# Windowed attention with a cosine feed-forward on one core: a pair's load one slot sooner, the scale of v one and two slots later

## The chip, the cores and the metric

The kernel runs on one core of a Trainium2 chip. The metric is the device time of one execution in microseconds (us). The engines of the core are PE (TensorE, matmuls; PEld is its weight load), DVE (VectorE), ACT (ScalarE), POOL (GpSimd) and SP (SyncE, which issues the DMAs here).

## The reference

Attention of 8 batches, 8 heads, 512 local and 32 global tokens of 64 dimensions; local queries see the global keys and a window of 32 to each side, global queries see all. Its output, 4608 tokens by 512, goes through a feed-forward layer whose activation is h cos(h):

```python
s_g = scale * np.matmul(q_g, k_all.transpose(0, 1, 3, 2))
out_g = np.matmul(sm(s_g), v_all)
s_ll = np.where(np.abs(pos[:, None] - pos[None, :]) <= 32, scale * q_l @ k_l^T, -1e9)
s_lg = scale * np.matmul(q_l, k_g.transpose(0, 1, 3, 2))
out_l = np.matmul(sm(np.concatenate([s_lg, s_ll], axis=-1)), np.concatenate([v_g, v_l], axis=2))
...
x = concatenate([out_g, out_l]) as (4608, 512)
h = x @ w_in            # 512 x 2048
out = (h * np.cos(h)) @ w_out   # 2048 x 512
```

## The kernel before, in words

Every fp32 operand of a product is scaled by a power of two and split into a high and a low fp16 part, and a product is three matmuls (high by high, high by low, low by high). Heads go in pairs: a batch has 4 pairs, 0 to 3. The feed-forward layer takes chunks of 256 tokens, two to a batch, and a chunk takes 8 steps (two 128-wide pieces of the 2048 each). A step is a *slot*, so a batch has 16 slots.

What belongs to a pair, by names and lines. `load_qk` (L457) fetches queries and keys, 608 KB, into `qkr`, of which there is one buffer. `qk_a` takes their largest magnitude, `qm` (L497, DVE). `qk_b` spreads it over the partitions through PE (`d_qk` L473 on DVE, `pm_qk` L479 on PE) and `qk_c` makes the scale `qs` of it. `qk_d` splits: `qa` (L537, ACT) and then `kl` (L538, DVE), the last reader of `qkr`. `qk_e` rearranges the parts by DMA (`kh<-qa`, L547 and L548; `qa<-kl`, L550; `kl<-kl`, L552). The scores `ps` are matmuls (L606, L607) in four windows, DVE masks them into `t` (L623, two halves to a window, with a maximum `mn`), ACT takes exponentials (L446), ACT and DVE write them out as `planes` (L702, L705), four DMA transposes a pair turn these into `pt` (L717), and PE multiplies them with v into `acc` (L750), which is split into `xh` (L775, ACT) and `xl` (L776, DVE). The global queries have their own scores (`gps`, `gt` L815), transposes (`ptg` L843) and product `gacc`.

What belongs to a batch's v: `load_v` (L464) fetches it, 1280 KB, into `vr` (one buffer). `v_a` takes the maximum `vm` (L566, DVE) and makes `d_v` (L473); `v_b` spreads it through PE (`pm_v`, L479); `v_c` takes the scale `vs` (L576 and three small instructions that follow it, DVE); `v_d` splits v of one pair, `vh` (L596, ACT) and `vl` (L597, DVE).

A step j of a chunk c: 24 matmuls `ph` (L919), `u` on ACT (L941) and DVE (L942), the sine `w` (ACT, L446), its square (POOL, L954), `gf` = (w - 0.5) ph (DVE, L956, the last reader of `ph`, which has 3 buffers), `gh` (ACT, L960), `gl` (POOL, L961), and matmuls `po` (L975 to L977). After a chunk, `o` (L983 on DVE, L985 on ACT) is written out. Exponential and sine need different tables on ACT, so an ACT_TABLE_LOAD stands between groups of them. The pieces of `w_out` are split in the same way in the first 250 us (L231, L268, L281).

What sets the order. The program is written as `at(slot, phase, function, arguments)`. Slot and phase give each call a priority; a list scheduler then places the instructions of each engine by priority and by its own estimate of when their operands are ready. Each engine, and SP with its DMAs, works through its own list in order. Names such as PF, PG, PA or PJ are phases inside a slot, from PA0, the first, to PJ, the last. For batch b from 2 on, t = 16 (b - 1) + T0 with T0 = 3, and pair p is placed around t + 4p: the load at `s_load`, the maximum at `s_qa` = -12, the splitting at `s_qd` = -10, the scores at -7 to -4, the transposes at -1, the product with v at 0, the splitting of v at -8. `s_v` = -12 places the load of v. Only pair 0 of batch 2 has a load of its own, at t - 11. In names with numbers, `qkr_4_0` is pair 0 of batch 4, `u_5_3` is step 3 of chunk 5, `t_3_3_2` is window 2 of pair 3 of batch 3; the last number only counts tiles.

Of the kernel before, what the change touches and what calls it, by code (L numbers as in the profile page):

```python
# [77 lines left out]
LVK = -1  # L78
LQK = -1
QMA = 2  # L80
s_load = -13
s_qa = -12
s_qd = -10
s_qe0 = -9
# [16 lines left out]
s_v = -12  # L101
# [36 lines left out]
def body(tc, qk, v, wi, wo, mask, out):  # L138
# [5 lines left out]
    with ExitStack() as ctx:  # L144
# [15 lines left out]
        for i in range(4):  # L160
            t = cp.tile([P, 2, 2, 256], F16, name=f"planes{i}")
# [844 lines left out]
        def at(slot, phase, f, *a, pr=None):  # L1006
            e = (phase, len(ev[slot]), f, a)
            ev[slot].append(e)
            pr = (slot, phase) if pr is None else pr if isinstance(pr, tuple) else (pr, phase)
            rank[slot, e[1]] = pr + (slot, e[1])  # L1010
# [3 lines left out]
        def attn_pair(b, p, o):  # L1014
            at(o["load"], PJ, load_qk, b, p)
            at(o["qa"], PF, qk_a, b, p)
            if o["tight"] or QB == 0:
                at(o["qa"], PG, qk_b, b, p)
                at(o["qa"], PG2, qk_c, b, p)
            else:  # L1020
                at(o["qa"] + 1, PA, qk_b, b, p)
                at(o["qa"] + 1, PB, qk_c, b, p)
            at(o["qd"], PF2, qk_d, b, p)
            for k in range(3):
                at(o["qe"][k], PA0 if k == 0 or o["tight"] else PJ, qk_e, b, p, k)
            for i in range(4):
                at(o["sc"][i], PA, sc_a, b, p, i)
                at(o["sc"][i], PA if o["tight"] else PC, sc_b, b, p, i)
                at(o["ex"], PI, sc_c, b, p, i)
                at(o["sd"], PF, sc_d, b, p, i)  # L1030
                at(o["tr"][i], PA2, sc_e, b, p, i)
            at(o["vd"], PF2, v_d, b, p)
            at(o["av"], PA, av_a, b, p)
            at(o["av"] if b else -6, PF, av_b, b, p)
            if p % 2:
                g = p // 2
                for k in range(2):
                    at(o["gs"][k], PA, g_a, b, g, k)
                    at(o["gs"][k], PA if o["tight"] else PC, g_b, b, g, k)
                at(o["ex"], PI, g_c, b, g)  # L1040
                at(o["gd"], PF2, g_d, b, g)
                at(o["ge"], PA2, g_e, b, g)
                at(o["gf"] if b else GF0, PG, g_f, b, g)
                at(o["gf"] if b else GF0, PH2, g_g, b, g)

        def steady(t, late=False):
            o = dict(
                load=t + s_load, qa=t + s_qa, qd=t + s_qd, qe=(t + s_qe0, t + s_qe1, t + s_qe2),
                sc=[t + s_sc0, t + s_sc1, t + s_sc2, t + s_sc3], ex=t + s_ex, sd=t + s_sd,
                tr=(t + s_tr,) * 4, vd=t + s_vd, av=t + s_av, gs=(t + s_gs0, t + s_gs1),  # L1050
                gd=t + s_gd, ge=t + s_ge, gf=t + s_gf, tight=False,
            )
            if late:
                o |= dict(load=t - 11, qa=t - 10, qd=t - 9, qe=(t - 8,) * 3)
            return o
# [45 lines left out]
        for b in range(2, B):  # L1101
            t = 16 * (b - 1) + T0
            at(t + s_v, PA0, load_v, b)
            at(t + s_v + 1, PF, v_a, b)
            at(t + s_v + 1, PG, v_b, b)
            at(t + s_v + 1, PG2, v_c, b)
            for p in range(NPAIR):
                attn_pair(b, p, steady(t + 4 * p, b == 2 and p == 0))
        ma, mb, mc, md, m2, ob, oc = (
# [99 lines left out]
```

## Time and profile before

| | before |
|---|---|
| median of 3 runs (lowest, highest) | 1033.6 us (1032.02, 1034.86) |
| the profiled execution | 1034.44 us, span 1032.6 us, mean granted clock 0.954 |
| busy: PE, PEld, DVE, ACT, POOL | 893.3, 609.2, 710.7, 717.9, 461.8 us |
| share of the chain that ended last | PE 33%, DVE 28%, ACT 15%, DMA 11%, POOL 5%, issue 5% |
| in that chain: DMA `qkr<-qk`, DVE `qm` | 7%, 2% |
| DMA | 120.19 MB, mean 116 GB/s |
| a `qkr` load | 608.0 KB, median 4.8 us from issue to landing |

Up to about 300 us the first two batches and the weights are prepared; up to about 814 us attention of batches 3 to 7 runs beside the feed-forward layer, at some 107 us a batch; behind that only the feed-forward layer is left. "Idle before" an instruction is time in which its engine stood still, and the name behind the arrow is what it waited for.

### The profile page before, as it was taken

The page shows a single profiled execution, that of the slowest core. Times are in us where ns is not written, and L with a number is a line of the kernel's source. Part 1 is how long each engine was busy: PE and PEld are TensorE (multiplying, and loading weights), DVE is VectorE, ACT ScalarE, POOL GpSimd, SP SyncE. Part 2 cuts the span into 40 slices and gives each one's busy share as a digit, 9 for nine tenths or more (in the row PEclk, how much of TensorE's full clock was granted, in tenths as well). Part 3 has the DMA queues.
Part 4 walks back from the last instruction along what each step waited for, and adds up shares of the span by engine and source line. Part 5 has one row for each costly group of instructions (what it writes and reads, how often), then busy time and mean ns, then how long its engine had stood idle before and what let it go on. Part 6 is the DMA issues. An engine that isn't in the chain of part 4 may idle for free.

```text
span 1032.6 us, 21117 instructions
## 1 busy us (share of the span) xinstructions
PE 893.3 (87%) x7947; PEld 609.2 (59%) x7947; DVE 710.7 (69%) x1811; ACT 717.9 (70%) x1468; POOL 461.8 (45%) x494
## 2 busy tenths in 40 slices
PE   1245878769999999899899999999989999999996
PEld 0134645444666766666666666666666667766663
DVE  4999786897477777867777777868777766433231
ACT  5788798785577776877687768777777876544342
POOL 3696477984233333333334324343333343534442
PEclk9996979788999999999999999999989999999998
DMA  9796145775254464454645354545536452100000
GB/s 361 269 303 246 15 142 142 181 164 139 70 103 111 103 157 108 99 115 97 147 93 119 91 145 93 122 91 153 111 81 109 107 88 61 34 21 22 1 21 21
DMA packets 165822, 120.19 MB, mean 116 GB/s; under 512 B 143064, under 2 KB 143064, under 8 KB 163672
## 3 DMA queue, kind: packets, MB, share of 16 engines
q1 hardware_dynamic: 165720, 118.85, 46.3%
q8 instruction: 62, 1.02, 0.4%
q14 instruction: 40, 0.33, 0.1%
HBM read 56.00 MB, written 8.91 MB: 63 GB/s over the span
## 4 chain that ended last, share of the span: by engine, by line
PE 33%; DVE 28%; ACT 15%; DMA 11%; POOL 5%; issue 5%; SPq 1%; ACTq 0%; DVEq 0%; POOLq 0%
PE ph L919 13%; DMA qkr<-qk 7%; PE po L975 5%; PE po L976 5%; PE po L977 5%; DVE planes L705 4%; DVE t L623 4%; DVE u L942 3%; ACT L446 3%; ACT planes L702 3%; ACT t L446 3%; DMA vr<-v 2%; DVE kl L538 2%; POOL w L954 2%; DVE qm L497 2%
## 5 line engine op out<-in xcount | busy, mean ns | idle before, releaser
L919 PE MATMUL ph<-xh,wi_h 128*128 128x256 f16 x1024 | 281.9, 276 | 10.0 <-DVE gf L956 9.8
L919 PE MATMUL ph<-xl,wi_h 128*128 128x256 f16 x1024 | 282.1, 275 | 0.0
L919 PE MATMUL ph<-xh,wi_l 128*128 128x256 f16 x1024 | 282.0, 275 | 0.0
L961 POOL TENSOR_TENSOR gl<-gf,gh 128x512 f16<-128x512 f32 x136 | 167.2, 1233 | 236.5 <-ACT gh L960 236.5
L954 POOL TENSOR_TENSOR w<-w 128x512 f32<-128x512 f32 x136 | 141.5, 1044 | 266.0 <-ACT w L446 266.0
L919 PEld LDWEIGHTS <-wi_h 128*128 128x128 f16 x2176 | 211.8, 99 | 52.3 <-issue 12.4
L975 PE MATMUL po<-wo_h,gh 128*128 128x512 f16 x544 | 206.5, 384 | 28.2 <-DVE o L983 17.1
L976 PE MATMUL po<-wo_l,gh 128*128 128x512 f16 x544 | 209.6, 385 | 10.6 <-POOL wo_l L231 10.6
L977 PE MATMUL po<-wo_h,gl 128*128 128x512 f16 x544 | 209.5, 386 | 0.0
L446 ACT ACTIVATE w<-u,ca 128x512 f32<-128x512 f32 x136 | 97.8, 721 | 109.9 <-DVE u L942 109.3
L942 DVE SCALAR_TENSOR_TENSOR u<-u,cm,ph 128x512 f32<-128x512 f32 x136 | 100.9, 742 | 97.3 <-ACT u L941 97.3
L446 ACT ACTIVATE t<-t,mn 128x192 f32<-128x192 f32 (+1 forms) x256 | 116.9, 458 | 49.3 <-DVE mn L623 48.9
L956 DVE SCALAR_TENSOR_TENSOR gf<-w,ph 128x512 f32<-128x512 f32 x136 | 92.6, 682 | 58.3 <-POOL w L954 58.1
L960 ACT CAST gh<-gf 128x512 f16<-128x512 f32 x136 | 83.1, 611 | 69.8 <-DVE gf L956 59.2
L919 PEld LDWEIGHTS <-wi_l 128*128 128x128 f16 x1088 | 107.5, 99 | 15.1 <-issue 1.4
L623 DVE CUSTOM_DVE_ANT_0 t<-ps,msk,al 128x192 f32<-128x192 f32 (+1 forms) x256 | 99.5, 426 | 11.7 <-PE ps L607 11.2
L941 ACT ACTIVATE u<-ph,cm 128x512 f32<-128x512 f32 x136 | 92.1, 678 | 21.4 <-PE ph L919 19.5
L977 PEld LDWEIGHTS <-gl 128*128 128x128 f16 x544 | 53.8, 99 | 75.5 <-issue 13.9
L705 DVE SCALAR_TENSOR_TENSOR planes<-t,sm,planes 128x224 f16<-128x224 f32 (+1 forms) x198 | 88.6, 496 | 10.7 <-ACT planes L702 10.7
L976 PEld LDWEIGHTS <-gh 128*128 128x128 f16 x544 | 53.7, 99 | 70.7 <-issue 22.7
L975 PEld LDWEIGHTS <-gh 128*128 128x128 f16 x544 | 53.1, 98 | 62.8 <-issue 14.5
L702 ACT ACTIVATE planes<-t,sm 128x192 f16<-128x192 f32 (+1 forms) x196 | 74.3, 453 | 0.0
(185 smaller groups left out, 1427.7 us busy)
## 6 DMA issues: line engine op xcount, KB each, us to landing
qkr<-qk SPq DMA_DIRECT2D x29, 608.0 KB, 4.8
vr<-v SPq DMA_DIRECT2D x8, 1280.0 KB, 7.7
kh<-qa SPq DMA_DIRECT2D x62, 152.0 KB, 2.6
out<-o SPq DMA_DIRECT2D x34, 256.0 KB, 2.7
raw_wm<-wo SPq DMA_DIRECT2D x16, 512.0 KB, 7.6
qa<-kl SPq DMA_DIRECT2D x31, 152.0 KB, 3.9
kl<-kl SPq DMA_DIRECT2D x31, 152.0 KB, 4.6
wo_h<-wi SPq DMA_DIRECT2D x4, 1024.0 KB, 6.7
```

What stands on the lines that cost most here:

```text
L446: ins = nc.scalar.activation(*a, **k).ins
L623: nc.vector.tensor_tensor_reduce(t[:, h], pt[:, h], msk[:, MOFF[i] : MOFF[i] + w], al, 3.0e38, ALU.add, ALU.min, mn[:, h : h + 1],)
L702: nc.scalar.activation(hi, t[:, h], AF.Identity, scale=r)
L705: nc.vector.scalar_tensor_tensor(lo, t[:, h], r, hi, op0=ALU.mult, op1=ALU.subtract)
L919: nc.tensor.matmul(ph[:, a], w[:, kc, f], x[:, kc, q], start=first and ip == 0, stop=last and ip == 2, skip_group_check=True,)
L942: nc.vector.scalar_tensor_tensor(u, u, m, ph, op0=ALU.subtract, op1=ALU.subtract)
L954: nc.gpsimd.tensor_tensor(w, w, w, op=ALU.mult)
L956: nc.vector.scalar_tensor_tensor(gf, w, 0.5, st.pop(("ph", c, j)).rearrange("p a b -> p (a b)"), op0=ALU.subtract, op1=ALU.mult,)
L961: nc.gpsimd.tensor_tensor(gl, gf, gh, op=ALU.subtract)
L975: nc.tensor.matmul(po[k], gh[:, q], wo_h[:, f], start=(f == 0), stop=False)
L976: nc.tensor.matmul(po[k], gh[:, q], wo_l[:, f], start=False, stop=False)
L977: nc.tensor.matmul(po[k], gl[:, q], wo_h[:, f], start=False, stop=(f == NJ - 1))
```

## The change

The load of queries and keys is given the slot -14 instead of -13, relative to the pair's place. For v of batches from 2 on, `v_a` (the maximum) goes one slot back, `v_b` and `v_c` (spread and scale) two slots; the load of v stays.

```diff
-s_load = -13
+s_load = -14
...
             at(t + s_v, PA0, load_v, b)
-            at(t + s_v + 1, PF, v_a, b)
-            at(t + s_v + 1, PG, v_b, b)
-            at(t + s_v + 1, PG2, v_c, b)
+            at(t + s_v + 2, PF, v_a, b)
+            at(t + s_v + 3, PA, v_b, b)
+            at(t + s_v + 3, PB, v_c, b)
```

SP at the load of pair 0 of batch 4, before:

```order
L548 DMA kh_3_3_5208<-qa_3_3_5204 64x1216
L843 DMA_TRANSPOSE ptg_3_0_5270<-planes_g_84 128x10x128
L550 DMA qa_3_3_5204<-kl_3_3_5205 64x1216
L717 DMA_TRANSPOSE pt_3_1_5265<-planes0_76 128x8x128
L717 DMA_TRANSPOSE pt_3_1_5265<-planes1_78 128x8x128
L717 DMA_TRANSPOSE pt_3_1_5265<-planes2_80 128x8x128
L717 DMA_TRANSPOSE pt_3_1_5265<-planes3_82 128x8x128
L457 DMA qkr_4_0_5277<-qk 128x1216
L552 DMA kl_3_3_5205<-kl_3_3_5205 64x1216
```

and now:

```order
L548 DMA kh_3_3_5208<-qa_3_3_5204 64x1216
L843 DMA_TRANSPOSE ptg_3_0_5272<-planes_g_84 128x10x128
L457 DMA qkr_4_0_5209<-qk 128x1216
L717 DMA_TRANSPOSE pt_3_1_5267<-planes0_76 128x8x128
L717 DMA_TRANSPOSE pt_3_1_5267<-planes1_78 128x8x128
L717 DMA_TRANSPOSE pt_3_1_5267<-planes2_80 128x8x128
L717 DMA_TRANSPOSE pt_3_1_5267<-planes3_82 128x8x128
L550 DMA qa_3_3_5204<-kl_3_3_5205 64x1216
L552 DMA kl_3_3_5205<-kl_3_3_5205 64x1216
```

The load moved ahead of the four transposes of pair 1 and of `qa<-kl`, and `qa<-kl` went behind the transposes. Pair 2 has the same move; at pairs 1 and 3 the load stands where it stood, right behind `kh`.

DVE at the same place, before (an ISA row with `t` is one half of a window's scores):

```order
L942 SCALAR_TENSOR_TENSOR u_4_5_5179<-u_4_5_5179,cm_4_4628,ph_4_5_5154 128x512
L623 ISA t_3_2_1_5200,mn_3_2_1_5201<-ps_3_2_1_5195,msk_73,al_3_2_4615 128x224
L623 ISA mn_3_2_1_5201 128x1
L623 ISA t_3_2_1_5200,mn_3_2_1_5201<-ps_3_2_1_5195,msk_73,al_3_2_4615 128x224
L623 ISA mn_3_2_1_5201 128x1
L956 SCALAR_TENSOR_TENSOR gf_4_4_5150<-w_4_4_5099,ph_4_4_5073 128x512
L956 SCALAR_TENSOR_TENSOR gf_4_5_5213<-w_4_5_5180,ph_4_5_5154 128x512
L942 SCALAR_TENSOR_TENSOR u_4_6_5242<-u_4_6_5242,cm_4_4628,ph_4_6_5217 128x512
L497 TENSOR_REDUCE qm_4_0_5377<-qkr_4_0_5277 128x1
```

and now:

```order
L942 SCALAR_TENSOR_TENSOR u_4_5_5179<-u_4_5_5179,cm_4_4628,ph_4_5_5154 128x512
L497 TENSOR_REDUCE qm_4_0_5377<-qkr_4_0_5209 128x1
L623 ISA t_3_2_1_5200,mn_3_2_1_5201<-ps_3_2_1_5195,msk_73,al_3_2_4615 128x224
L623 ISA mn_3_2_1_5201 128x1
L623 ISA t_3_2_1_5200,mn_3_2_1_5201<-ps_3_2_1_5195,msk_73,al_3_2_4615 128x224
L623 ISA mn_3_2_1_5201 128x1
L956 SCALAR_TENSOR_TENSOR gf_4_4_5150<-w_4_4_5099,ph_4_4_5073 128x512
L196 TENSOR_SCALAR qm_4_0_5377<-qm_4_0_5377 128x1
L956 SCALAR_TENSOR_TENSOR gf_4_5_5215<-w_4_5_5180,ph_4_5_5154 128x512
L473 TENSOR_SCALAR d_qk4_0_5380<-ident_64,qm_4_0_5377 128x128
L473 TENSOR_SCALAR d_v4_5566<-ident_64,vm_4_5564 128x128
L942 SCALAR_TENSOR_TENSOR u_4_6_5244<-u_4_6_5244,cm_4_4628,ph_4_6_5219 128x512
```

The maximum `qm` moved from behind `u_4_6` to right behind `u_4_5`, and the two diagonals (`d_qk`, `d_v`) with it. Pair 2 has the same move, without `d_v`.

DVE where v of batch 4 is split, before:

```order
L538 SCALAR_TENSOR_TENSOR kl_4_0_5576<-qkr_4_0_5277,qs_4_0_5388,qa_4_0_5575 128x1216
L868 TENSOR_SCALAR xg_99<-gacc_3_0_5580,pvs_100 128x2x32
L597 SCALAR_TENSOR_TENSOR vl_4_1_6160<-vr_4_5328,vs_4_5502,vh_4_1_6159 128x640
L597 SCALAR_TENSOR_TENSOR vl_4_2_6596<-vr_4_5328,vs_4_5502,vh_4_2_6595 128x640
L942 SCALAR_TENSOR_TENSOR u_5_2_5675<-u_5_2_5675,cm_4_4628,ph_5_2_5650 128x512
L497 TENSOR_REDUCE qm_4_1_5814<-qkr_4_1_5712 128x1
```

and now (the place is a slot later):

```order
L484 TENSOR_SCALAR vs_4_5704<-vs_4_5704 128x1
L942 SCALAR_TENSOR_TENSOR u_5_3_5749<-u_5_3_5749,cm_4_4628,ph_5_3_5724 128x512
L597 SCALAR_TENSOR_TENSOR vl_4_0_5820<-vr_4_5328,vs_4_5704,vh_4_0_5819 128x640
L597 SCALAR_TENSOR_TENSOR vl_4_1_6160<-vr_4_5328,vs_4_5704,vh_4_1_6159 128x640
L597 SCALAR_TENSOR_TENSOR vl_4_2_6596<-vr_4_5328,vs_4_5704,vh_4_2_6595 128x640
L623 ISA t_3_3_2_5709,mn_3_3_3_5809<-ps_3_3_3_5804,msk_73,al_3_3_5051 128x192
```

`vl_4_0` came from ahead of `kl_4_0`, `vl_4_1` and `vl_4_2` from right behind it, and all three now stand between `u_5_3` and the scores of the last window of pair 3. The three `vh` on ACT moved with them, to right behind the ACT part of `u_5_3`. In the passage from batch 1 to batch 2, around 190 to 250 us, many instructions of all engines change places.

## The prediction

> **What bounds the kernel now.** I read the busy shares first, then the stages, the waits of the steady stage, and at last the timelines of the two places that the change touches.
>
> ```profile
> PE 893.3 (87%) x7947; PEld 609.2 (59%) x7947; DVE 710.7 (69%) x1811; ACT 717.9 (70%) x1468; POOL 461.8 (45%) x494
> ```
>
> ```profile
> 300.00:814.00 514.00, 485.40 (x4530) 335.02 (x4528) 387.89 (x1009) 383.49 (x816) 185.97 (x163) 0.98 0.50 113
> 814.00:1032.60 218.60, 208.76 (x1655) 140.62 (x1654) 89.23 (x187) 108.57 (x203) 85.41 (x77) 0.98 0.16 35
> ```
>
> The columns are the window, its length, then the busy time and instructions of PE, PEld, DVE, ACT and POOL, the clock, the DMA share and GB/s. Batches 3 to 7 are prepared from 300 to 814 us. There PE is idle for 514.00 - 485.40 = 28.6 us; DVE and ACT are about three quarters busy, yet they hand work to each other one piece at a time. This chain of hand-overs bounds the stage. From 814 us on attention is done and PE works off the rest, where the change has nothing to do.
>
> The waits between 300 and 900 us (total us, how often, longest):
>
> ```profile
> DVE qm L497 <- DMA qkr<-qk: 47.5, 20, 4.0
> PE po L975 <- DVE o L983: 17.1, 10, 3.0
> ```
>
> The largest is VectorE's wait for queries and keys, at the maximum qm. The question is how much of it the chain feels.
>
> **The earlier load.** In the order of instructions it moves only for pairs 0 and 2 of a batch (ten times in batches 3 to 7, and pair 2 of batch 2). It passes five issues on SP, `qa<-kl` and four transposes. Here is pair 0 of batch 4, SP first:
>
> ```profile
> 397.68 1.37 SPq L843 DMA_TRANSPOSE ptg<-planes_g  x1
> 400.30 5.51 SPq L717 DMA_TRANSPOSE pt<-planes  x4
> 405.86 0.57 SPq L457 DMA_DIRECT2D qkr<-qk  x1
> ```
>
> Then VectorE, with the wait ahead of an instruction in brackets:
>
> ```profile
> 396.48 2.34 DVE L538 SCALAR_TENSOR_TENSOR kl<-qkr,qs,qa 128x1216 f16<-128x1216 f32 x1 [1.62 <-ACT qa L537]
> 403.68 0.73 DVE L942 SCALAR_TENSOR_TENSOR u<-u,cm,ph 128x512 f32<-128x512 f32 x1
> 404.33 0.44 DVE L623 CUSTOM_DVE_ANT_0 t<-ps,msk,al 128x224 f32<-128x224 f32 x1
> 405.39 0.69 DVE L956 SCALAR_TENSOR_TENSOR gf<-w,ph 128x512 f32<-128x512 f32 x1 [0.24 <-POOL w L954]
> 407.35 0.75 DVE L942 SCALAR_TENSOR_TENSOR u<-u,cm,ph 128x512 f32<-128x512 f32 x1 [0.28 <-ACT u L941]
> 410.79 1.42 DVE L497 TENSOR_REDUCE qm<-qkr 128x1 f32<-128x1216 f32 x1 [2.70 <-DMA qkr<-qk]
> ```
>
> The buffer is free when kl ends, at 396.48 + 2.34 = 398.82; SP issues the load at 405.86, and qm starts 4.93 us later. In the new order it follows ptg: 397.68 + 1.37 = 399.05. With the same 4.93 us it lands near 404.0. qm also moves on VectorE, from behind u_·_6 to right behind u_·_5, which ends at 403.68 + 0.73 = 404.41. So I expect almost no wait. But qm (1.42 us) now stands ahead of two halves of t and of gf. The halves take about 0.8 us (404.33 to 405.39 less 0.24), so gf starts at 404.41 + 1.42 + 0.8 = 406.6 instead of 405.39: 1.2 us late. ScalarE queues behind it:
>
> ```profile
> 406.11 0.62 ACT L960 CAST gh<-gf 128x512 f16<-128x512 f32 x1 [0.88 <-DVE gf L956]
> 406.64 0.68 ACT L941 ACTIVATE u<-ph,cm 128x512 f32<-128x512 f32 x1
> 408.19 0.72 ACT L446 ACTIVATE w<-u,ca 128x512 f32<-128x512 f32 x1 [0.37 <-DVE u L942]
> 412.62 0.48 ACT L446 ACTIVATE t<-t,mn 128x224 f32<-128x224 f32 x1 [0.47 <-DVE mn L623]
> ```
>
> gh goes to about 407.3, u to 407.8, VectorE's u to 408.5, w to 409.3, 1.1 us late, and the table load and the first exponentials with it. What the chain gets back is ScalarE's idle time ahead of the third exponential, which waited for the scores that stood behind qm; here it is 0.47. Over the ten places it is 1.75 in the first, 1.15 in the last, and 10.0 us in all (1.75, .32, .47, 1.48, .77, 1.32, .91, 1.27, .58, 1.15):
>
> ```profile
> 305.19 0.48 ACT L446 ACTIVATE t<-t,mn 128x224 f32<-128x224 f32 x1 [1.75 <-DVE mn L623]
> 788.77 0.48 ACT L446 ACTIVATE t<-t,mn 128x224 f32<-128x224 f32 x1 [1.15 <-DVE mn L623]
> ```
>
> So the 32 us that these ten waits for the load take are worth 10.0, and qm's new place costs 10 x 1.1 = 11: together +1.0. Bounds: -10 if the lateness of gf costs nothing, and +11 if the load lands 1 us after VectorE arrives, since the DMA engines are full there with transposes:
>
> ```profile
> 403.00:405.00 2.00, 2.00 (x13) 1.03 (x11) 2.00 (x6) 1.22 (x2) 0.68 (x1) 1.00 1.03 201
> ```
>
> I take the +1.0, since 4.93 us was measured with those transposes still landing. Moved behind them, `qa<-kl` lands some 6 us later; it feeds the scores of the next pair only slots afterwards: nothing. The odd pairs' loads already stood right behind kl.
>
> PE's wait for gf at this place grows from 0.91 to about 2.1:
>
> ```profile
> 406.14 0.28 PE L919 MATMUL ph<-xh,wi_h 128*128 128x256 f16 x1 [0.91 <-DVE gf L956]
> 438.94 0.59 PE L975 MATMUL po<-wo_h,gh 128*128 128x512 f16 x1 [2.19 <-DVE o L983]
> 438.90:442.30 3.40, 3.36 (x24) 1.42 (x25) 2.33 (x8) 2.46 (x8) 1.16 (x1) 0.50 0.23 83
> ```
>
> Behind the 2.19 us gap the clock stands at 0.50 for 3.4 us, 1.7 us of work lost. Such a loss may follow the new gap too, but it is PE's time, and PE has 28.6 us to spare: nothing in the sum, something in the upper bound. The Trainium skill, page "TensorE: Matmul & The Clock Gate", section "Why this matters for your kernels", has the clock drop only for idle gaps above about 3 us; by that rule the new gap costs nothing at all. The trace differs, with half clock behind 2.19 us, and decides.
>
> **The later spread of v.** Once per batch. Before, one piece of splitting v (vh, vl) stood ahead of kl, and two right behind it:
>
> ```profile
> 432.01 0.35 SPq L457 DMA_DIRECT2D qkr<-qk  x1
> 432.09 2.39 DVE L597 SCALAR_TENSOR_TENSOR vl<-vr,vs,vh 128x640 f16<-128x640 f32 x2
> 434.40 0.74 DVE L942 SCALAR_TENSOR_TENSOR u<-u,cm,ph 128x512 f32<-128x512 f32 x1
> 436.81 1.42 DVE L497 TENSOR_REDUCE qm<-qkr 128x1 f32<-128x1216 f32 x1 [1.67 <-DMA qkr<-qk]
> ```
>
> There VectorE had to wait for the next load anyway, so the 2.39 us come free: taking them away only makes that wait longer. All three pieces and the scale vs move behind u_·_3, ahead of the last two halves of t:
>
> ```profile
> 440.85 0.68 ACT L941 ACTIVATE u<-ph,cm 128x512 f32<-128x512 f32 x1
> 428.98 1.53 ACT L596 ACTIVATE vh<-vr,vs 128x640 f16<-128x640 f32 x2
> 441.56 0.75 DVE L942 SCALAR_TENSOR_TENSOR u<-u,cm,ph 128x512 f32<-128x512 f32 x1 [1.07 <-ACT u L941]
> 443.73 0.42 DVE L623 CUSTOM_DVE_ANT_0 t<-ps,msk,al 128x192 f32<-128x192 f32 x1 [1.42 <-PE ps L607]
> 548.82 0.75 DVE L942 SCALAR_TENSOR_TENSOR u<-u,cm,ph 128x512 f32<-128x512 f32 x1 [1.34 <-ACT u L941]
> 549.48 0.41 DVE L623 CUSTOM_DVE_ANT_0 t<-ps,msk,al 128x192 f32<-128x192 f32 x1
> 766.51 0.42 DVE L623 CUSTOM_DVE_ANT_0 t<-ps,msk,al 128x192 f32<-128x192 f32 x1 [2.53 <-PE ps L607]
> L597 DVE SCALAR_TENSOR_TENSOR vl<-vr,vs,vh x19: 872/1577/1801, 319.6 to 755.0; 128x640 f16<-128x640 f32 x19
> 441.02 1.16 POOL L961 TENSOR_TENSOR gl<-gf,gh 128x512 f16<-128x512 f32 x1 [4.01 <-ACT gh L960]
> ```
>
> Three vh take 3 x 0.81 = 2.4 us from 441.53 to 443.96, and the last vl (0.88; least, median and longest are 872, 1577 and 1801 ns, and POOL is free from 442.18) then ends near 445.0. The halves of t start there, not at 443.73: +1.2 us, partly covered by the 1.42 that they waited. Where that wait is nil, as at 549.48, they are 2.6 late; where it is 2.53, as at 766.51, nothing. Over batches 3 to 7: 1.3 + 1.2 + 2.6 + 2.6 + 0 = 7.7. Then comes a rigid row: last exponentials, table load, w, qa, kl, next load. Gained is the vs part ahead of gf_·_0, up to 0.64 us of the path (425.08 to 425.72), which mostly ends in the unchanged wait for the load; I take 0.2 a batch, 1.0 in all. Sum +6.7; bounds -3 (all lateness absorbed, 0.6 gained) and +17 (each vl at 1.58).
>
> **The passage from batch 1 to 2.** Around 190 to 250 us the order of all engines is shuffled: splitting v of batch 2 comes later, pieces of w_out sooner, pair 3 of batch 1 later.
>
> ```profile
> 190.00:210.00 20.00, 15.19 (x127) 9.97 (x127) 15.26 (x40) 15.20 (x32) 17.39 (x26) 0.67 0.86 201
> 210.00:230.00 20.00, 11.07 (x150) 7.07 (x147) 18.20 (x44) 18.67 (x41) 15.57 (x20) 0.85 0.67 157
> 230.00:250.00 20.00, 17.89 (x168) 9.59 (x167) 18.87 (x51) 12.14 (x27) 10.43 (x14) 0.73 0.70 136
> ```
>
> PE is idle there for 60 - 44.15 = 15.9 us with VectorE nearly full. I can't tell the sign: 0, with a guess of a quarter of those 15.9, 4 us, either way.
>
> Sum: 1.0 + 6.7 + 0 = +7.7. The profiled execution took 1034.44 us, its span 1032.6, and the median is 1033.6; on the median this gives 1041.3, so 1041.
>
> **Rivals.**
> A, other side, faster: gf's lateness is taken up by slack (ScalarE waits for VectorE and PE elsewhere), and so is v's, so that only the 10.0 us of ScalarE's idle time are left: 1033.6 - 10 = 1023.6. It decides if qkr lands before u_·_5 ends and gf passes on less than 0.3 us of its 1.2. For it speaks the size of the waits; against it that gh, u and w stand without slack behind gf (waits of 0.88 and 0.37).
> B, no change: v is absorbed where PE waits for o and VectorE anyway (17.1 us at po), and the passage offsets the rest: within 3 us, 1034.
> C, late load: the load shares the DMA engines with four transposes, lands 1 us after VectorE comes to qm, and that wait now stands ahead of gf: 10 more, 1051. For it the full DMA engines; against it the 4.93 us.
> D, dear vl: the three vl meet POOL's instructions and take 1.58: 5 x 3 x 0.7 = 10.5 more, 1052. Against it stands POOL's free time after 442.18. The Trainium skill, page "SBUF — State Buffer", section "Who interferes with whom", says that a VectorE instruction with two SBUF inputs contends with a GpSimd instruction that reads SBUF, and that one is blocked fully. The trace agrees (872 against 1577 ns).
>
> **Numbers.** This kernel's runs scatter by about 0.3%, 3 us. The forecast has 0.42, its own range 1037 to 1047. A 0.26, B 0.20, C 0.07, D 0.05. Slower is 0.42 + 0.07 + 0.05 = 0.54, same 0.20, faster 0.26. The range leaves out the far part of A, and of C and D: 1026 to 1050.
>
> **What would show it.** Even pairs: qkr's issue right behind ptg, qm's wait below 0.5, gf 1.2 us later against u_·_5, ScalarE's 0.5 to 1.7 ahead of the third exponential gone. First odd pair: qm's wait grows from 1.67 to about 3.5, since the two vl that filled the time left. v's place: vl at 0.88, three in a row behind u_·_3, and t behind them with no wait for PE. The window 300 to 814, cut at the same events, some 8 us longer, PE idle 36. The prediction is wrong if w and the exponentials keep their distance from u_·_5 though gf is late, or if the passage moves more than 4 us.

## The result, and the profile after

The change made the kernel slower: 1045.62 us (1043.61 to 1046.99) against 1032.81 us, a ratio of 1.0113 with a 95% interval of 1.0088 to 1.0137. The forecast was 1041, some 8 us more; measured are 12 to 13.

The page of the kernel after:

```profile
span 1042.6 us, 21108 instructions
PE 893.4 (86%) x7947; PEld 609.3 (58%) x7947; DVE 712.4 (68%) x1811; ACT 716.4 (69%) x1468; POOL 458.9 (44%) x494
```

The same work takes 10.0 us more of span, so the time is idle time. It arises in the steady stage. Both windows below run from the end of the `kl` that frees `qkr` for pair 0 of batch 3 to the end of the one that frees it for pair 3 of batch 7, first before, then after:

```profile
290.12:808.29 518.17, 490.60 (x4563) 338.25 (x4561) 392.24 (x1027) 385.45 (x818) 189.20 (x166) 0.98 0.51 113
```

```profile
290.30:818.41 528.11, 493.26 (x4558) 339.45 (x4557) 390.74 (x1028) 384.11 (x817) 187.22 (x166) 0.98 0.50 111
```

It starts at the same time (290.12 and 290.30), so the passage from batch 1 to 2, though reshuffled, cost nothing in these two traces. It is 9.9 us longer, and PE is idle for 34.9 us instead of 27.6.

Now the place of the earlier load, pair 0 of batch 4, in the kernel after; SP, VectorE, ScalarE:

```profile
398.46 1.37 SPq L843 DMA_TRANSPOSE ptg<-planes_g  x1
399.87 0.74 SPq L457 DMA_DIRECT2D qkr<-qk  x1
400.88 6.60 SPq L717 DMA_TRANSPOSE pt<-planes  x4
```

```profile
404.45 0.73 DVE L942 SCALAR_TENSOR_TENSOR u<-u,cm,ph 128x512 f32<-128x512 f32 x1
405.11 1.40 DVE L497 TENSOR_REDUCE qm<-qkr 128x1 f32<-128x1216 f32 x1
407.18 0.67 DVE L956 SCALAR_TENSOR_TENSOR gf<-w,ph 128x512 f32<-128x512 f32 x1
408.63 1.18 DVE L473 TENSOR_SCALAR d_v<-ident,vm 128x128 bf16<-128x128 f32 x1
409.74 0.73 DVE L942 SCALAR_TENSOR_TENSOR u<-u,cm,ph 128x512 f32<-128x512 f32 x1
```

```profile
407.88 0.62 ACT L960 CAST gh<-gf 128x512 f16<-128x512 f32 x1 [1.88 <-DVE gf L956]
410.57 0.72 ACT L446 ACTIVATE w<-u,ca 128x512 f32<-128x512 f32 x1 [0.97 <-DVE u L942]
```

The load goes out right behind `ptg`, and `qm` no longer waits. But gf starts 2.0 us behind the end of u (405.18) where it was 1.0 before (404.41 to 405.39), and ScalarE's wait for it grows from 0.88 to 1.88. So where `DVE qm <- DMA qkr` shrinks, another wait grows; from 290 to 820 us after:

```profile
DVE qm L497 <- DMA qkr<-qk: 29.5, 11, 4.9
ACT gh L960 <- DVE gf L956: 32.9, 20, 3.3
```

Before, from 290 to 810 us, these were 45.9 and 9.2 us. Not all of the growth of the second is the load's: with the load alone (below) it is 20.2 us, and with v alone 19.9, since `vh` no longer stands ahead of gh on ScalarE. And the place where v is split, VectorE and ScalarE:

```profile
437.73 1.42 DVE L497 TENSOR_REDUCE qm<-qkr 128x1 f32<-128x1216 f32 x1 [3.77 <-DMA qkr<-qk]
442.68 0.75 DVE L942 SCALAR_TENSOR_TENSOR u<-u,cm,ph 128x512 f32<-128x512 f32 x1 [0.89 <-ACT u L941]
443.40 2.48 DVE L597 SCALAR_TENSOR_TENSOR vl<-vr,vs,vh 128x640 f16<-128x640 f32 x3
445.79 0.41 DVE L623 CUSTOM_DVE_ANT_0 t<-ps,msk,al 128x192 f32<-128x192 f32 x1
```

```profile
442.55 2.25 ACT L596 ACTIVATE vh<-vr,vs 128x640 f16<-128x640 f32 x3
446.25 0.45 ACT L446 ACTIVATE t<-t,mn 128x192 f32<-128x192 f32 x1 [0.87 <-DVE mn L623]
```

The three `vl` stand in a row between u and t. Before, t came 1.4 us behind the end of that u, having waited for PE; now it comes 2.4 us behind it, and the exponential waits for it. And `qm` of the odd pair waits 3.77 us instead of 1.67, since the two `vl` that had filled that time are gone.

### The profile page after: what moved, and what is told of

Same layout as the page of the kernel before. It is cut to its first block, busy times and chain, and to the rows that moved or that the text cites. A ratio compares the mean times of both kernels' runs of the same rounds, so it can differ in the third digit from the quotient of the medians.

```text
span 1042.6 us, 21108 instructions
## 1 busy us (share of the span) xinstructions
PE 893.4 (86%) x7947; PEld 609.3 (58%) x7947; DVE 712.4 (68%) x1811; ACT 716.4 (69%) x1468; POOL 458.9 (44%) x494
## 4 chain that ended last, share of the span: by engine, by line
PE 36%; DVE 27%; ACT 15%; DMA 11%; POOL 6%; issue 5%; SPq 0%; ACTq 0%; POOLq 0%; DVEq 0%
PE ph L919 16%; DMA qkr<-qk 6%; PE po L975 5%; PE po L976 5%; PE po L977 5%; DVE t L623 3%; DMA vr<-v 3%; ACT L446 3%; ACT t L446 3%; DVE u L942 3%; DVE gf L956 2%; DVE planes L705 2%; DVE kl L538 2%; POOL w L954 2%; DVE qm L497 2%
## 5 line engine op out<-in xcount | busy, mean ns | idle before, releaser
L919 PE MATMUL ph<-xh,wi_h 128*128 128x256 f16 x1024 | 283.4, 277 | 17.0 <-DVE qm L196 10.7
L977 PEld LDWEIGHTS <-gl 128*128 128x128 f16 x544 | 53.5, 98 | 73.7 <-issue 11.7
```

The costliest lines, as they stand in the source:

```text
L919: nc.tensor.matmul(ph[:, a], w[:, kc, f], x[:, kc, q], start=first and ip == 0, stop=last and ip == 2, skip_group_check=True,)
L977: nc.tensor.matmul(po[k], gl[:, q], wo_h[:, f], start=False, stop=(f == NJ - 1))
```

## The experiments

To compare the runs I cut each trace at the ends of the `kl`, four steps to a batch. Step A ends with `kl` of pair 0 and holds the even pair's `qm` and, before, the scale vs with the first `vl`. Step B ends with `kl` of pair 1 and holds the place where v is now split. Step C ends with `kl` of pair 2 (the other even pair), step D with that of pair 3. Sums over batches 3 to 7 (D: four of them), in us, from one trace each:

| kernel | A | B | C | D | all | ratio (95% interval) |
|---|---|---|---|---|---|---|
| before | 168.7 | 95.3 | 169.8 | 84.4 | 518.2 | 1 |
| before, second trace | 169.8 | 95.0 | 170.2 | 86.9 | 522.0 | 1.0001 (0.9979 to 1.0024) |
| after | 169.2 | 103.7 | 169.4 | 85.9 | 528.1 | 1.0113 (1.0088 to 1.0137) |
| after, second trace | 169.2 | 103.3 | 170.8 | 89.5 | 532.8 | 1.0086 (1.0060 to 1.0112) |
| load alone | 171.5 | 95.6 | 168.5 | 86.9 | 522.5 | 1.0021 (1.0001 to 1.0040) |
| v alone | 165.5 | 102.1 | 169.7 | 88.7 | 526.0 | 1.0033 (1.0016 to 1.0051) |
| v pieces alone | 166.7 | 100.2 | 168.5 | 86.5 | 521.8 | 1.0021 (1.0006 to 1.0037) |
| v alone, vl behind the scores | 165.5 | 92.7 | 170.3 | 86.2 | 514.8 | 0.9952 (0.9930 to 0.9974) |
| load, qm held | 162.9 | 94.0 | 163.2 | 87.2 | 507.2 | 0.9869 (0.9846 to 0.9892) |
| whole change, qm held | 159.6 | 102.1 | 163.2 | 87.5 | 512.4 | 0.9910 (0.9886 to 0.9935) |
| load, qm held, odd pair too | 162.9 | 86.4 | 164.2 | 89.4 | 502.9 | 0.9839 (0.9814 to 0.9864) |
| scale off the path | 158.3 | 137.8 | 131.0 | 86.6 | 513.6 | 0.9986 (0.9963 to 1.0008) |

The experiments ran on three chips, where the kernel before took 1036 to 1038 us; each ratio is to the kernel before on the same chip, so the ratios are compared, not the times. A trace is of one execution; those of the whole change run once more (1050.12 us, "after, second trace") and of the whole change with qm held (1031.86 us) were the longest of their six.

**The kernel before, unchanged.** This run tells how far single steps scatter.

> The kernel before as it is, for a second trace of it: it tells how much of a step's time from trace to trace is scatter. Ratio 1.000; the steps from one kl to the next within 0.3 us of the first trace, if single steps may be compared; up to 2 us apart where PE's half clock falls otherwise.

A, B and C agree within 1.2 us in their sums, but a single step of B differed by up to 2.8 us: the 0.3 us did not hold, and single steps are not compared. D differs by 2.5, also between the two traces of the kernel after (3.6), so nothing is read from D, and nothing below 1.5 from A, B or C.

**The load alone.**

```diff
-s_load = -13
+s_load = -14
```

> Only the earlier load (slot -14), v as before. Theory (the three vh and vl ahead of the last scores make the loss, and the earlier load gives back with gf's lateness what it gains): 1033 to 1036, no change. Rival 1 (the earlier load makes the loss, by qm standing ahead of gf): about 1045, as the whole change. Rival 2 (the load alone is a gain that v eats up): 1024 to 1028.

It measured 1.0021 (1.0001 to 1.0040). As the theory said, next to nothing: the wait of the ten even `qm` fell from 32.3 us to 0.6 and the time did not fall at all. A and C together are 340.0 against 338.5 and 340.1.

**v alone.** Maximum one slot, spread and scale two slots later, load as before.

> Only v later (maximum one slot, spread and scale two), load as before. Theory: the whole loss of the change, 1041 to 1046. Rival 1 (the loss is in the load): 1031 to 1035. Rival 2: above 1050, since the load then gave some back.

It measured 1.0033 (1.0016 to 1.0051), 1040.9 against 1036.3 us. This is a loss, but not the whole one that the theory asked for. The table shows two opposite terms: B grows by 7.0 us, and A falls by 3.7 (both against the mean of the two traces of before).

**The pieces alone.** The scale stays early, and only `vh` and `vl` of pairs 0 to 2 go to the new place:

```diff
+                if b > 2 and p < 3:
+                    tc.add_manual_dep(i1.ins, st["u_act"].name, order, reason="pieces_late")
+                    tc.add_manual_dep(i2.ins, st["u_dve"].name, order, reason="pieces_late")
+                    st["vl_i", b] = i2.ins
...
-            at(o["vd"], PF2, v_d, b, p)
+            late = b > 2 and p < 3
+            at(o["vd"] - 4 * p if late else o["vd"], PB if late else PF2, v_d, b, p)
...
+                if p == 3 and i == 3 and h == 0 and ("vl_i", b + 1) in st:
+                    tc.add_manual_dep(tt.ins, st["vl_i", b + 1].name, order, reason="t_behind_vl")
```

> The kernel before, load, maximum, spread and scale of v where they were; only vh and vl of pairs 0 to 2, batches 3 to 7, are put behind u of step 3 and ahead of the last window of pair 3, where the change has them. Theory: their place is the cost, the same loss as the whole of v, 1040 to 1044. Rival (the later scale, the other order of PE or the passage from batch 1 to 2 makes the loss): 1031 to 1035.

It measured 1.0021 (1.0006 to 1.0037), 1039.2 against 1036.3 us: a loss of about 2 to 3 us, less than half of what I expected. Its B (+5.0) and A (-2.5) have the signs of v alone. Behind u of step 3 it loses as much as v alone: from the start of that u to the start of `kl` the five batches take 42.7 us in both kernels, against 36.0 and 35.1 in the two traces of before. Ahead of that u it is 2 us shorter than v alone, where the scale now stands. So the pieces' place makes the growth of B.

**The load with qm held.** The load as early as in the change, but `qm` keeps its old place behind u of step 6:

```diff
+            st["us"] = st.get("us", []) + [i2.ins.name]
...
+                if p % 2 == 0 and (b, p) != (2, 0):
+                    tc.add_manual_dep(red.ins, st["us"][-2], order, reason="qm_behind_u")
```

> The earlier load alone, but qm is held behind u of step 6 on VectorE, where it stood before, so that gf is not late. Theory: the 10.0 us of ScalarE's idle time ahead of the third exponential of ten pairs come free without the price, 1023 to 1027. Rival (that idle time is not on the path, something else ends last): 1031 to 1035, as with the earlier load alone.

It measured 0.9869 (0.9846 to 0.9892), 1023.4 us. Its trace at pair 0 of batch 4, VectorE and ScalarE:

```profile
400.22 0.69 DVE L959 SCALAR_TENSOR_TENSOR gf<-w,ph 128x512 f32<-128x512 f32 x1 [0.24 <-POOL w L957]
402.18 0.75 DVE L944 SCALAR_TENSOR_TENSOR u<-u,cm,ph 128x512 f32<-128x512 f32 x1 [0.28 <-ACT u L943]
402.84 1.41 DVE L497 TENSOR_REDUCE qm<-qkr 128x1 f32<-128x1216 f32 x1
```

```profile
400.94 0.62 ACT L963 CAST gh<-gf 128x512 f16<-128x512 f32 x1 [0.89 <-DVE gf L959]
403.02 0.72 ACT L446 ACTIVATE w<-u,ca 128x512 f32<-128x512 f32 x1 [0.37 <-DVE u L944]
```

The waits of gh and w are those of before (0.88 and 0.37), `qm` waits for nothing, and A and C together fall by 12.5 and 14.0 us against the two traces of before. Through the steady stage ScalarE, GpSimd and SP work in the same order as with the load alone; only VectorE's and PE's order differ, with `qm` and the spread that follows it. So the removed wait is worth 13 us, and the same load without the held `qm` gives all of it back. This is rival A of the prediction, in the form that its condition names: gf not late.

**The whole change once more.**

> The whole change once more, on the chip of the parts, since its parts came out at 1.0021 and 1.0033 and the whole at 1.0113. If the parts simply add up and the first chip only stood differently: a ratio of 1.004 to 1.007. If the two parts make each other worse: 1.010 to 1.013 here too.

It measured 1.0086 (1.0060 to 1.0112), between the two cases; it ran on another chip than the parts. The product of the parts is 1.0054. The interval of the whole touches what the parts' intervals allow, so that they make each other worse is possible and not shown.

**The whole change with qm held.**

> The whole change, with qm held behind u of step 6 as in the run before. Theory (the places of qm and of the v pieces cost independently): the gain of the held qm, 13 us, and the loss of the v pieces, 4 to 8 us, together 1026 to 1031 if the kernel before takes 1035. Rival (the later v is only dear while gf is late as well): 1022 to 1025.

It measured 0.9910 (0.9886 to 0.9935), 1027.6 us. v costs a ratio of 1.0042 beside the held `qm` (0.9910 to 0.9869) and 1.0033 beside the old load. The intervals are wider than the difference, so this agrees with the theory and does not prove it. In the trace B is 102.1 us, as with v alone, against 94.0 with the held `qm`: v's price in B is there without gf's lateness, against the rival.

**v alone, with vl behind the scores.** As v alone, but

```diff
+                if b > 2 and p < 3:
+                    tc.add_manual_dep(i2.ins, st["rr_i", b - 1, 3].name, order, reason="vl_behind_rr")
...
-            at(o["vd"], PF2, v_d, b, p)
+            at(o["vd"] + (2 if b > 2 and p == 0 else 0), PF2, v_d, b, p)
```

where `rr_i` is the reciprocal that follows the scores on VectorE.

> v alone later, as in the run with 1.0033, but the three vl are put behind the scores of the last window, between the scale of the next pair and its kl, where VectorE waited 1.6 us for qa; the three vh stay ahead of the last exponentials on ScalarE. Theory (vl's place makes t late and that is the cost): the step with the pieces, 20.4 us on average with v late and 19.0 to 19.1 before, falls to about 19.5, and the ratio to 0.998 to 1.001. Rival (the 2.4 us of vh on ScalarE hold xh and the exponentials as long): the step stays at 20 or more, ratio 1.002 to 1.005.

It measured 0.9952 (0.9930 to 0.9974), better than the theory asked for: B falls by 9.4 us against v alone, 1.9 a step. Its trace:

```profile
442.04 0.41 DVE L625 CUSTOM_DVE_ANT_0 t<-ps,msk,al 128x192 f32<-128x192 f32 x1
445.73 1.63 DVE L597 SCALAR_TENSOR_TENSOR vl<-vr,vs,vh 128x640 f16<-128x640 f32 x2
448.95 1.49 DVE L538 SCALAR_TENSOR_TENSOR kl<-qkr,qs,qa 128x1216 f16<-128x1216 f32 x1 [0.66 <-ACT qa L537]
```

t stands right behind u again, and from the start of that u to the start of `kl` the five batches take 37.3 us instead of 42.7. Besides, `kl` takes 1.49 us here and 2.34 before, since a GpSimd instruction moved from beside it to behind it; the five of them are 4.3 of the 9.4 us. Together with the pieces alone this shows the place of `vl` ahead of t as the cause of B's growth. The gain in the ratio is that 4.3 and the shorter A, and not the edit alone: the scheduler also moved pair 2's load ahead of the transposes and its `qm` ahead of gf. The wait of that `qm` fell from 16.6 us in C to none, and C did not fall (169.7 and 170.3): the wait was worth nothing there too.

**The odd pair too.** On top of the held `qm`, `qm` of the first odd pair goes behind the scores of window 2 and gf of step 2, and two `vl` behind `qm`:

```diff
+                if p == 1 and b > 2:
+                    tc.add_manual_dep(red.ins, st["gf"].name, order, reason="qm_behind_gf")
+                    st["red", b] = red.ins
...
+                if b > 2 and p in (1, 2):
+                    tc.add_manual_dep(i2.ins, st["red", b].name, order, reason="vl_behind_qm")
```

> The earlier load with held qm, v as before, and at the first odd pair of a batch qm is put behind the scores of window 2 and gf of step 2, and the second and third vl behind qm, so that neither o, scores nor gf wait for the load there. Theory (ScalarE's 2.77 us wait for u and the 1.9 us wait for the load at this pair are on the path): 1.5 to 3 us a batch less than 1023.4, 1008 to 1016. Rival (PE, idle only 21 us from 300 to 830, or ScalarE takes over): 1019 to 1023.

It measured 0.9839 (0.9814 to 0.9864), 1020.0 us, the lowest of all, but its interval overlaps that of the held `qm` alone, and the time is on the rival's side. B fell by 7.6 us as meant, while C and D grew by 3.3 in the one trace, no more than these sums scatter. PE is idle for 22.3 of its 502.9 us:

```profile
289.97:792.84 502.87, 480.56 (x4557) 332.86 (x4556) 392.59 (x1027) 383.97 (x817) 190.38 (x166) 1.00 0.54 116
```

Where the rest of the 7.6 us went was not traced further.

**Scale off the path.** On top of that, maximum, spread and scale of v one slot later, all pieces behind `qm` of pair 1:

```diff
-            at(t + s_v + 1, PF, v_a, b)
-            at(t + s_v + 1, PG, v_b, b)
-            at(t + s_v + 1, PG2, v_c, b)
+            at(t + s_v + 2, PF, v_a, b)
+            at(t + s_v + 2, PG, v_b, b)
+            at(t + s_v + 2, PG2, v_c, b)
```

> The fastest version so far (early load, held qm, 1020 us), with the maximum, spread and scale of v all one slot later: vs comes behind kl of pair 0, off the path that leads to it, and all three vl come behind qm of pair 1; the three vh stand ahead of u of step 2 on ScalarE. Theory: the step that lost vs and one vl is 0.64 us shorter in each of five batches, 3.2 in all, if the three vh cost nothing where ScalarE waits for u: 1016 to 1018. Rival (vh ahead of u delays w of step 2 by up to 2.4 us a batch): 1022 to 1030.

It measured 0.9986 (0.9963 to 1.0008), 1037.1 us, far beyond the rival. Neither of the two reasons is what the trace shows: the scheduler also put the steps from `qm` to the scale qs of that pair later, and `qa` waited for qs (12.3 us in the five steps B). Against the run above, B grew by 51.4 us in the sum while A and C fell by 37.8, and the stage began 6.2 us later (296.2 against 290.0).

## Why the prediction was right, and where it was off

The sign, the range and the mechanism held: chain of hand-overs, a removed DMA wait that buys nothing because `qm` then stands ahead of gf, and pieces of v that move to a place ahead of t. That the number came near is in part luck: the load's gain and loss were both some 3 us larger than forecast and cancel, a gain of 3 us from v was missed, and the whole change lost more than its parts. By its steps:

- *Load right behind ptg, almost no wait.* 399.87 behind 399.83, and the ten waits of `qm` are 2.2 us in all (3.7 in the second trace, 0.6 with the load alone). The late load (rival C) came in small only: at two places of the ten, three in the second trace, the load took 6.1 to 6.6 us to land instead of about 5, `qm` waited 0.8 to 1.3 us, and the step was longer by as much. Pair 0 of batch 6 has the longest of these waits. The dear vl (rival D) did not come: vl takes 0.88 at the new place (2.48 for three in a row).

```profile
625.60 1.42 DVE L497 TENSOR_REDUCE qm<-qkr 128x1 f32<-128x1216 f32 x1 [1.29 <-DMA qkr<-qk]
```

- *10.0 gained, 11 lost, together +1.0.* The sum held (load alone: A and C +0.7 against the mean of before, ratio 1.0021), but both terms were too small. The loss can be read between the end of `kl` and the table load ahead of the exponentials: 10.1 us at all ten places before and with the held `qm`; with the load alone 11.1 to 11.4 at pair 2 and 11.7 at pair 0 (12.25 once, where `qm` waited 0.45). That is 13.9 us in all, and A and C are 14.0 longer than with the held `qm`. So gf's lateness costs 1.0 a place, close to the 1.1 of the forecast. The 0.6 that pair 0 pays on top is a price that I did not have: the diagonal `d_v` takes 1.2 us at its new place instead of 0.3, and w waits 0.97 for u instead of 0.37. The gain is 12.5 to 14.0 us. ScalarE's idle time ahead of the third exponential makes 10.0 of it, 11.7 in the second trace, and is gone; what else came sooner was not traced. The table load at pair 0 of batch 4, in the kernel before, with the load alone and with the held `qm`, where `kl` ended at 398.82, 397.49 and 393.66:

```profile
408.93 1.28 ACT L446 ACT_TABLE_LOAD   x1
409.20 1.28 ACT L446 ACT_TABLE_LOAD   x1
403.76 1.28 ACT L446 ACT_TABLE_LOAD   x1
```

- *PE's wait for gf from 0.91 to about 2.1.* Here the step failed, without weight for the sum: at the same place it is 0.89, and 10.7 us in eight places, 1.7 at most (the releaser named stands right behind gf):

```profile
407.91 0.28 PE L919 MATMUL ph<-xh,wi_h 128*128 128x256 f16 x1 [0.89 <-DVE qm L196]
PE ph L919 <- DVE qm L196: 10.7, 8, 1.7
```

- *t late by 7.7.* It held. t starts 2.3 to 2.4 us behind u in all five batches, with v alone and with the whole change, where it was 0 to 2.5 before; that is 6.7 us more than in the first trace of before and 7.7 more than in the second, and `kl` starts as much later. B grew by 7.0 with v alone and by 8.3 in the two traces of the whole change. (The scale vs came to stand ahead of u of step 3, not behind it.)
- *Gained ahead of gf 0.2 a batch, 1.0 in all.* Here the prediction left out a term. A fell by 3.7 us with v alone. Ahead of gf the gain is only 0.5 in all: without vs, gf waits 0.52 us for GpSimd's w. But the first piece, which stood between that gf and the next, is gone too, and the way from gf to gf falls from 4.2 or 4.6 us to 3.6, by 3.3 us in the five batches. With the pieces alone, where vs stays, it falls just so. The prediction counted that piece as work that moves and gave nothing for the place that it left. The two gf and the piece in batch 4, before:

```profile
425.72 0.68 DVE L956 SCALAR_TENSOR_TENSOR gf<-w,ph 128x512 f32<-128x512 f32 x1
426.97 0.88 DVE L597 SCALAR_TENSOR_TENSOR vl<-vr,vs,vh 128x640 f16<-128x640 f32 x1
429.90 0.69 DVE L956 SCALAR_TENSOR_TENSOR gf<-w,ph 128x512 f32<-128x512 f32 x1 [0.66 <-POOL w L954]
```

and with v alone:

```profile
424.97 0.69 DVE L956 SCALAR_TENSOR_TENSOR gf<-w,ph 128x512 f32<-128x512 f32 x1 [0.52 <-POOL w L954]
428.58 0.69 DVE L956 SCALAR_TENSOR_TENSOR gf<-w,ph 128x512 f32<-128x512 f32 x1 [1.05 <-POOL w L954]
```

I thought the wait for the next load would eat such a gain; but that load starts at the end of `kl`, so an earlier `kl` carries it along.
- *Passage: 0, with 4 us either way.* The steady stage starts at 290.1 and 290.7 before, at 290.3 and 291.3 after.
- *Odd pair's wait from 1.67 to about 3.5.* 3.77 at that place, 19.8 us in the five batches against 7.7.

These terms give 0.7 + 7.0 - 3.7 = 4.0 us; the product of the parts' ratios, 5.6 us, agrees with that within the scatter. The whole change cost 9 to 12 us. The traces show two places for the rest. The waits of `qm` that came back make 1.6 and 3.1 us more in A and C than with the load alone; without them the whole change has 167.9 and 167.8 in A, 168.5 and 168.4 in C, within 0.6 of what the two parts add up to. And the steady stage starts at 288.3 with the load alone and at 288.7 with v alone, some 2 us sooner than before, but not with both. This is read from one or two traces of each kernel, and why the passage differs is open.

## What to carry to other kernels

A long wait in the table of waits is worth only what its removal brings forward on the chain: here 30 us of DMA wait were worth nothing when the waiting instruction came to stand ahead of a hand-over to another engine, and 13 us when it kept its place. When a load is moved sooner, look where its consumer goes in the engine's own order, and pin the consumer if the scheduler moves it up. And work that sits in a wait is free there, like the two `vl` behind `kl`: move it out only when the new place is free too. The first piece, ahead of `kl`, was not free, and moving it away gained 3 us.

## What the runs showed of the hardware

Some VectorE instructions took longer beside a GpSimd instruction, also a small one. The diagonal `d_v` (128x128) in the kernels before and after:

```profile
L473 DVE TENSOR_SCALAR d_v<-ident,vm x8: 278/282/705, 45.0 to 734.6; 128x128 bf16<-128x128 f32 x8
```

```profile
L473 DVE TENSOR_SCALAR d_v<-ident,vm x8: 515/1187/1197, 44.1 to 738.3; 128x128 bf16<-128x128 f32 x8
408.58 2.27 POOL L961 TENSOR_TENSOR gl<-gf,gh 128x512 f16<-128x512 f32 x2 [1.45 <-ACT gh L960]
```

After, it starts at 408.63, just behind a GpSimd instruction that starts at 408.58, and takes 1.18 us instead of 0.28; it ends when that instruction has ended (the row holds two of them, of 1.16 us each). Not every instruction does so: u starts at 409.74, just behind the second of them (409.69), and takes 0.73 us, no longer than elsewhere. `kl` is the same story before, beside the low part of the global planes:

```profile
449.01 1.22 POOL L839 TENSOR_TENSOR planes_g<-gt,planes_g 128x544 f16<-128x544 f32 x1
449.17 2.34 DVE L538 SCALAR_TENSOR_TENSOR kl<-qkr,qs,qa 128x1216 f16<-128x1216 f32 x1 [1.62 <-ACT qa L537]
```

It took 2.34 us there and 1.49 where that instruction had moved behind it. The Trainium skill, page "SBUF — State Buffer", section "Who interferes with whom", says that VectorE and GpSimd share a port pair as an exclusive lock, for VectorE instructions with two SBUF inputs and for those in a mode that takes both ports, and that the one that comes second blocks fully. The traces agree for `d_v`, which lost 0.9 us, though no run shows in which mode it works; `kl` lost 0.85 of the 1.06 us that it ran beside the other.
